# Products with w_ch2 by Strassen's algorithm inside each group of 288 tokens

## Chip, core and metric

The kernel runs on one core of a Trainium2 chip. The metric is the device time of one execution in microseconds (us). The kernel before takes 1440.85 us (median of 3 runs, 1440.07 to 1442.34). The core has five engines that work side by side: TensorE (PE, products into the PSUM banks), VectorE (DVE), ScalarE (ACT), GpSimd (POOL), and SyncE (SP), which here only issues DMA.

## What is computed

Attention with a threshold, over 8 batches, 8 heads, 576 tokens and 64 dimensions a head, and then a feed-forward block on the 512 features of each token:

```python
scores = (q @ k.T) / 8
scores = where(scores >= max(scores) - tau, scores, -1e9)
attn = exp(scores - max(scores)); attn /= sum(attn) + 1e-9
x = (attn @ v), heads side by side                        # (8, 576, 512)
xn = (x - mean(x)) / sqrt(var(x) + 1e-6) * g_ln
out = x + maximum(xn @ w_ch1, 0) @ w_ch2                  # 512 -> 2048 -> 512
```

Everything is float32. The change concerns the last product, with w_ch2, of 2048 hidden values by 512 features.

## The kernel before

The 4608 tokens are worked in 16 groups of 288 (TOK), two to a batch. The attention of a batch is cut into 9 slots (SLOTS). A slot takes the scores of a pair of heads for 256 rows of queries (one slot of the nine takes the rows left over), in two PSUM tiles sc0 and sc1. The feed-forward products of a finished group are spread over the slots that follow, as filler between the slot's own products, in four portions ("quarters") per slot. Constants: NK = 4 blocks of 128 features, ND = 16 blocks of 128 hidden values, B = 8, HP = 4.

A product of 128 x 128 weights is issued as two matmuls of 64 output columns each:

```python
    def product(out, lhsT, rhs, **flags):
        for h in range(2):
            r = slice(64 * h, 64 * h + 64)
            nc.tensor.matmul(out[r], lhsT=lhsT[:, r], rhs=rhs, **flags)
```

The attention of a slot: maxima (neg, on DVE), exponentials (ACT), threshold and sums (DVE), division (POOL), block transposes (DVE), and a way through memory that finishes the transposition (SP). From the second batch on all slots go this way.

```python
        # exponentials(): neg, thr, and es = att.tile(..., tag="e"), two buffers
            nc.vector.tensor_reduce(out=neg[:, i], in_=pairs[h], axis=AXL.X, op=ALU.max, negate=True)
            # ... thr on POOL ...
            nc.scalar.activation(es[:, i], blocks[i], func=AF.Exp, bias=neg[:, i : i + 1])
        # weights():
            nc.vector.scalar_tensor_tensor(out=es[:, i], in0=blocks[i], scalar=thr[:, i : i + 1],
                in1=es[:, i], op0=ALU.is_ge, op1=ALU.mult, accum_out=den[:, i : i + 1])
        nc.vector.reciprocal(den, den)
            nc.gpsimd.tensor_scalar(out=es[:, i], in0=es[:, i], scalar1=den[:, i : i + 1], ...)
        # turn_blocks(): two transposes per slot into et (one buffer), then to memory
                    nc.vector.transpose(et[...], es[:, 2 * h : 2 * h + 2]...)
            nc.sync.dma_start(out=scr[:, :, a]..., in_=et[32 * a : 32 * a + 32])   # 4 of them
        # fetch(), in the next slot:
        nc.sync.dma_start(out=em, in_=rows[: J * 128]...)
        nc.sync.dma_start(out=er[:64], in_=rows[J * 128 :])        # the tile "rest"
        # values_of(), in the next slot's last quarter: em and rest times v, into sc0's free columns
```

When a group's x is complete, its mean is taken by a product with a constant matrix, and DVE centres x:

```python
    def centre(g):
        xc = centred[g] = ffn.tile([128, NK, TOK], F32, tag="xc", bufs=1, name="xc")
        for c in range(NK):
            nc.vector.tensor_tensor(out=xc[:, c], in0=groups[g][:, c], in1=mean, op=ALU.subtract)
```

The feed-forward block of a group is a generator. ps_ff has two PSUM banks; p1, p2, mean, var and the segments of the change share them. Things for other engines that need not be issued at once are appended to the list aside, which the main loop empties four times per slot.

```python
    def ffn_steps(g):
        for d in range(ND):
            p1 = ps_ff.tile([128, TOK], F32, tag="ff", name="p1")
            for c in range(NK):
                product(p1, lhsT=w1_sb[c][:, d * 128 : (d + 1) * 128], rhs=xc[:, c], ...)
                # yield 1 after each: one step of the filler
            nc.scalar.activation(hidden[:, d], p1, func=AF.Relu)
            # d == 1: squares of xc into sq, summed on POOL; d >= 8: product var with avg_sb, and
            # root() by three steps on DVE: rb = 1 / sqrt(var + eps)
        for m in range(NK):
            p2 = ps_ff.tile([128, TOK], F32, tag="ff", name="p2")
            for d in range(ND):
                product(p2, lhsT=w2_sb[:, m, d], rhs=hidden[:, d], start=(d == 0), stop=(d == ND - 1))
            aside.append(lambda m=m, p2=p2: add_to_x(g, m, p2, rb))

    def add_to_x(g, m, p2, rb):
        o = ffn.tile([128, TOK], F32, tag="o", bufs=6, name="o")
        nc.vector.tensor_mul(o, p2, rb)
        nc.gpsimd.tensor_tensor(out=o, in0=o, in1=groups[g][:, m], op=ALU.add)
        aside.append(lambda: store(g, m, o))     # a DVE transpose into ot, then four DMA to out
```

The pace: ROOM gives the share of each quarter, and what is left of a group's steps is spread evenly until the next group is ready. Within a slot the order is: scores; neg; two exponentials; quarter 0; two exponentials; transposes of the next heads' q and k (kT, qT), if any; aside; quarter 1; weights(); aside; quarter 2; turn_blocks(); aside; quarter 3 with the values' product ahead of it; aside.

## Time and profile before

| engine | busy us | share of the span of 1438.0 us |
|---|---|---|
| PE | 1389.3 | 97% |
| DVE | 868.9 | 60% |
| POOL | 439.0 | 31% |
| ACT | 421.7 | 29% |

The page of the profile gives the busy time of each engine, the chain of work that ended last, and groups of instructions by line; the timeline lists instructions in order of time. A row of a group gives line, engine, operation, output and inputs, shape, count, busy time, the mean of one in ns, and the engine's idle time just before it with what ended it. In a timeline row the bracket at the end gives the idle time ahead of the instruction and what released it. The products with w_ch2 are named p<-hidden,w, those with w_ch1 p<-xc,w; the scores are sc<-kT,qT, the values sc<-em,v_in. In the last 20 us PE runs alone with the last group's products: 31.21 us for 256 records of p<-hidden,w, and the span ends some 6 us after them.

### The profile page before, as it was taken

What the parts mean: (1) busy time and instruction counts of PE and PEld (TensorE: products, weight loads), DVE (VectorE), ACT (ScalarE), POOL (GpSimd) and SP (SyncE); (2) the same over time, 40 slices, a digit from 0 to 9 for tenths busy, and PEclk for the clock granted to TensorE, in tenths of its full rate; (3) what the DMA queues carried; (4) which work ended last, traced back from release to release, by engine and by line L of the source; (5) the groups of instructions that cost most, each with busy time, mean ns of one, the idle gap of its engine ahead of it and who ended that gap; (6) DMA issues with size and microseconds to landing.
All of it is one profiled execution on the core that took longest, in us unless ns stands there. A gap on an engine that the chain in (4) does not pass through costs nothing.

```text
span 1438.0 us, 29661 instructions
## 1 busy us (share of the span) xinstructions
PE 1389.3 (97%) x12168; PEld 851.0 (59%) x12168; DVE 868.9 (60%) x1492; ACT 421.7 (29%) x818; POOL 439.0 (31%) x681
## 2 busy tenths in 40 slices
PE   4879999999999999999999999999999999999998
PEld 3655665655656555655556555565556555565664
DVE  5997957556665666566665565656665666655111
ACT  3886523132221313132221312213131222213020
POOL 2344432333323233232322333232332323222100
PEclk8999999999999999999999999999999999999999
DMA  9722456658755586557865577555875578455301
GB/s 223 176 69 83 90 137 157 168 136 168 178 145 145 144 185 166 142 134 168 184 156 145 146 160 168 144 145 144 175 179 146 130 168 185 135 145 137 79 6 17
DMA packets 466840, 205.12 MB, mean 143 GB/s; under 512 B 275024, under 2 KB 428368, under 8 KB 466704
## 3 DMA queue, kind: packets, MB, share of 16 engines
q1 hardware_dynamic: 461936, 202.64, 58.6%
q8 instruction: 95, 1.56, 0.5%
q10 hardware_dynamic: 4736, 0.59, 0.4%
q14 instruction: 41, 0.34, 0.1%
q0 software_dynamic: 32, 0.00, 0.0%
HBM read 119.41 MB, written 83.76 MB: 141 GB/s over the span
## 4 chain that ended last, share of the span: by engine, by line
PE 89%; DVE 5%; ACT 2%; DMA 2%; issue 1%; SPq 1%; POOL 0%; POOLq 0%; DVEq 0%; ACTq 0%
PE p L100 67%; PE sc L538 10%; PE sc L384 10%; DVE e L416 1%; PE tp L100 1%; DMA v_in<-in_v_dram 1%; DVE neg L398 1%; SPq L115 1%; ACT e L409 1%; PE mean L100 0%; DVE et L494 0%; DVE w L263 0%; PE var L100 0%; DMA qk_room<-in_q_dram 0%; ACT hidden L649 0%
## 5 line engine op out<-in xcount | busy, mean ns | idle before, releaser
L100 PE MATMUL p<-xc,w 128*64 128x288 f32 x4096 | 517.9, 408 | 6.6 <-ACT hidden L649 4.5
L100 PE MATMUL p<-hidden,w 128*64 128x288 f32 x4096 | 513.9, 407 | 0.0
L100 PEld LDWEIGHTS p<-xc,w 128*64 128x64 f32 x4096 | 292.6, 137 | 216.0 <-ACT hidden L649 14.5
L100 PEld LDWEIGHTS p<-hidden,w 128*64 128x64 f32 x4096 | 293.3, 137 | 200.6 <-issue 9.3
L398 DVE TENSOR_REDUCE neg<-sc 128x2 f32<-128x1152 f32 x144 | 188.8, 1353 | 252.1 <-PE sc L384 252.1
L409 ACT ACTIVATE e<-sc,neg 128x576 f32<-128x576 f32 x288 | 194.6, 742 | 261.3 <-DVE neg L398 255.9
L429 POOL TENSOR_SCALAR e<-e,den 128x576 f32<-128x576 f32 x252 | 188.3, 766 | 242.6 <-DVE den L420 242.6
L416 DVE SCALAR_TENSOR_TENSOR e<-sc,thr,e 128x576 f32<-128x576 f32 x288 | 219.1, 811 | 24.2 <-ACT e L409 24.2
L494 DVE STREAM_TRANSPOSE et<-e 128x1152 f32<-128x1152 f32 x112 | 153.6, 1375 | 78.2 <-POOL e L429 52.1
L649 ACT ACTIVATE hidden<-p 128x288 f32<-128x288 f32 x256 | 105.7, 414 | 284.7 <-PE p L100 282.9
L384 PE MATMUL sc<-kT,qT 64*128 64x384 f32 (+3 forms) x1024 | 150.0, 424 | 20.9 <-DVE e L416 10.8
L402 POOL TENSOR_SCALAR thr<-neg,low_sb 128x2 f32<-128x2 f32 x144 | 41.8, 291 | 352.9 <-DVE neg L398 344.0
L384 PEld LDWEIGHTS sc<-kT,qT 64*128 64x128 f32 x1024 | 94.1, 190 | 77.9 <-issue 26.8
L538 PE MATMUL sc<-em,v_in 128*64 128x256 f32 (+1 forms) x1408 | 131.1, 330 | 2.6 <-DVE sq L627 1.2
L555 ACT COPY x<-sc 128x256 f32<-128x256 f32 x60 | 22.3, 372 | 314.6 <-PE sc L538 289.6
L538 PEld LDWEIGHTS sc<-em,v_in 128*64 128x64 f32 x1408 | 86.2, 138 | 42.1 <-issue 1.7
L597 POOL TENSOR_TENSOR o<-o,x 128x288 f32<-128x288 f32 x64 | 51.6, 806 | 151.5 <-DVE o L596 151.5
L596 DVE TENSOR_TENSOR o<-p,rb 128x288 f32<-128x288 f32 x64 | 28.1, 439 | 103.1 <-PE p L100 102.5
L564 POOL TENSOR_TENSOR sum<-sum,x 128x256 f32<-128x256 f32 (+1 forms) x64 | 32.9, 514 | 76.8 <-ACT x L555 74.3
L655 POOL TENSOR_TENSOR sq<-sq 128x288 f32<-128x288 f32 x48 | 38.8, 807 | 42.1 <-ACT sq L653 39.6
L564 POOL TENSOR_TENSOR sum<-x 128x256 f32<-128x256 f32 (+1 forms) x32 | 16.2, 507 | 96.5 <-ACT x L555 55.1
L538 PE MATMUL sc<-rest,v_rest 128*64 128x256 f32 (+1 forms) x352 | 44.4, 329 | 0.0
(130 smaller groups left out, 713.9 us busy)
## 6 DMA issues: line engine op xcount, KB each, us to landing
scr<-et SPq DMA_DIRECT2D x252, 288.0 KB, 4.8
em<-scr SPq DMA_DIRECT2D x63, 1024.0 KB, 5.9
out_dram<-ot SPq DMA_DIRECT2D x256, 36.0 KB, 4.4
q_in<-in_q_dram SPq DMA_DIRECT2D x124, 72.0 KB, 3.3
k_in<-in_k_dram SPq DMA_DIRECT2D x120, 72.0 KB, 2.8
v_in<-in_v_dram SPq DMA_DIRECT2D x64, 128.0 KB, 4.4
rest<-scr SPq DMA_DIRECT2D x63, 128.0 KB, 5.9
w<-in_moe_w_ch_dram SPq DMA_DIRECT2D x10, 512.0 KB, 6.8
```

Source lines behind the costliest of these rows:

```text
L100: nc.tensor.matmul(out[r], lhsT=lhsT[:, r], rhs=rhs, **flags)
L384: nc.tensor.matmul(sc[h][64 * i : 64 * i + 64 if s == HP else 128, at : at + n], lhsT=ql[r] if s == HP else qT[r, half, j * 128 : (j + 1) ...
L398: nc.vector.tensor_reduce(out=neg[:, i], in_=pairs[h], axis=AXL.X, op=ALU.max, negate=True,)
L402: nc.gpsimd.tensor_scalar(out=thr[:, i], in0=neg[:, i], scalar1=-1.0, scalar2=low_sb, op0=ALU.mult, op1=ALU.add,)
L409: nc.scalar.activation(es[:, i], blocks[i], func=AF.Exp, bias=neg[:, i : i + 1])
L416: nc.vector.scalar_tensor_tensor(out=es[:, i], in0=blocks[i], scalar=thr[:, i : i + 1], in1=es[:, i], op0=ALU.is_ge, op1=ALU.mult, accum_o ...
L429: nc.gpsimd.tensor_scalar(out=es[:, i], in0=es[:, i], scalar1=den[:, i : i + 1], scalar2=1.0, op0=ALU.mult, op1=ALU.mult,)
L494: nc.vector.transpose(et[:, :, 64 * h : 64 * h + 64].rearrange("p n (j c) -> p j n c", j=2), es[:, 2 * h : 2 * h + 2].rearrange("p j (n c) ...
L538: nc.tensor.matmul(dst[64 * h : 64 * h + 64], lhsT=vt[:, c, h, :] if c < J else vr[:, h, :], rhs=pick(em[:, c] if c < J else er, hp, h), s ...
L564: nc.gpsimd.tensor_tensor(out=sums[g][:, cols], in0=x[:, 0, cols] if c == 1 else sums[g][:, cols], in1=x[:, c, cols], op=ALU.add,)
L597: nc.gpsimd.tensor_tensor(out=o, in0=o, in1=groups[g][:, m], op=ALU.add)
L649: nc.scalar.activation(hidden[:, d], p1, func=AF.Relu)
```

## The change

Strassen's algorithm (in Winograd's form) multiplies two matrices cut into 2 x 2 blocks by 7 block products in place of 8, at the price of sums and differences of blocks. Here w_ch2 is cut by halves of the output features and of the hidden values, and hidden by halves of the hidden values and of the tokens (early and late, 144 each). The first group (g = 0) stays as it was; from the second on (g >= 1) each group takes seven "segments" of 16 products with 144 moving columns. A segment accumulates two blocks of features in one PSUM bank, and ACT copies it out.

The sums of weights are made once, during the first products of group 1: s1 in place of a block of w_ch2, s2 and s3 in the staging tile of the weights' conversion, s4 in one of the two rooms for e (so the attention has a single room for e from then on). The differences of hidden (t1 to t4) are made per group, in place in hidden, by DVE (t1, t2) and POOL (t3, t4). POOL adds the seven results up (u2, u3, u4, 11, 12, 21, 22), DVE multiplies by rb, POOL adds x, and the result is transposed and stored as before. The steps' count and the places of the squares and of var within the first product are adapted. The aim is fewer products on the engine that is busiest.

```diff
@@ -88,6 +88,7 @@
     rests = [consts.tile([128, 4, 128], F32, name=f"rest{i}") for i in range(2)]
     v_rest = [consts.tile([128, 2, D], F32, name=f"v_rest{i}") for i in range(HP)]
     hidden = consts.tile([128, ND, TOK], F32, name="hidden")
+    e_room = [consts.tile([128, 4, S], F32, name=f"e{i}") for i in range(2)]
# ... the weights' staging tile is kept as self.stage ...
 
-    def exponentials():
+    def exponentials(n):
 
 
         neg = small.tile([128, 4], F32, tag="neg", name="neg")
         thr = small.tile([128, 4], F32, tag="thr", name="thr")
-        es = att.tile([128, 4, S], F32, tag="e", name="e")
+        es = e_room[(n + 1) % 2 if n < SLOTS else 0]
         for h in range(2):
             i = slice(2 * h, 2 * h + 2)
# ...
@@ -629,15 +630,47 @@
         if step < 2:
             aside.append(lambda: root(y, x, t, step + 1))
 
-    def ffn_steps(g):
-
+    HT, HD, HM = TOK // 2, ND // 2, NK // 2
+    early, late = slice(0, HT), slice(HT, TOK)
+    w2 = {
+        (i, j): w2_sb[:, HM * i : HM * i + HM, HD * j : HD * j + HD]
+        for i in range(2)
+        for j in range(2)
+    }
+    more = []
+
+    def differences():
+
+
+        flat = conversion.stage.rearrange("p a b -> p (a b)")
+        flat4 = e_room[1].rearrange("p a b -> p (a b)")
+        size = HM * HD * 128
+        for t in (flat[:, :size], flat[:, size : 2 * size], flat4[:, :size]):
+            more.append(t.rearrange("p (m d c) -> p m d c", m=HM, d=HD))
+        s2, s3, s4 = more
+        s1 = w2[1, 0]
+        for eng, out, a, b, op in (
+            (nc.gpsimd, s3, w2[0, 0], w2[1, 0], ALU.subtract),
+            (nc.vector, s1, w2[1, 0], w2[1, 1], ALU.add),
+            (nc.vector, s2, s1, w2[0, 0], ALU.subtract),
+            (nc.gpsimd, s4, w2[0, 1], s2, ALU.subtract),
+        ):
+            for m in range(HM):
+                for d in range(0, HD, 4):
+                    at = (slice(None), m, slice(d, d + 4))
+                    eng.tensor_tensor(out=out[at], in0=a[at], in1=b[at], op=op)
+                    yield
+
+    def first_part(g):
 
 
         xc = centred.pop(g)
-        rb = None
+        rb = sq = None
+        plain = g == 0
+        sums_of = differences() if g == 1 else iter(())
         for d in range(ND):
             while conversion.ended < 4 * (d // 4 + 1):
-                yield 0
+                yield 0, 0
             p1 = ps_ff.tile([128, TOK], F32, tag="ff", name="p1")
             for c in range(NK):
                 product(
@@ -645,35 +678,145 @@
                     start=(c == 0), stop=(c == NK - 1),
                 )
                 if c < NK - 1:
-                    yield 1
+                    yield 1, 1
             nc.scalar.activation(hidden[:, d], p1, func=AF.Relu)
-            yield 2
-            if d == 1:
+            next(sums_of, None)
+            yield 2, 1
+            if d == (1 if plain else 5):
                 sq = ffn.tile([128, NK, TOK], F32, tag="sq", bufs=1, name="sq")
                 nc.scalar.activation(sq, xc, func=AF.Square)
                 for c in range(1, NK):
                     nc.gpsimd.tensor_tensor(out=sq[:, 0], in0=sq[:, 0], in1=sq[:, c], op=ALU.add)
-            if d >= 8 and rb is None and (part or d == ND - 1):
+            if d >= (8 if plain else 11) and rb is None and (part or d == ND - 1):
 
                 var = ps_ff.tile([128, TOK], F32, tag="ff", name="var")
                 product(var, lhsT=avg_sb, rhs=sq[:, 0], start=True, stop=True)
                 rb = ffn.tile([128, TOK], F32, tag="rb", bufs=2, name="rb")
                 nc.scalar.activation(sq[:, 1], var, func=AF.Identity, bias=eps_sb)
                 aside.append(lambda: root(rb, sq[:, 1], sq[:, 2]))
-                yield 1
+                yield 1, 1
+        for _ in sums_of:
+            pass
+        return rb
+
+    def second_plain(g, rb):
         for m in range(NK):
             p2 = ps_ff.tile([128, TOK], F32, tag="ff", name="p2")
             for d in range(ND):
                 while conversion.ended <= conversion.n1 + 4 * m + d // 4:
-                    yield 0
+                    yield 0, 0
                 product(
                     p2, lhsT=w2_sb[:, m, d], rhs=hidden[:, d],
                     start=(d == 0), stop=(d == ND - 1),
                 )
                 if d < ND - 1:
-                    yield 2
+                    yield 2, 1
             aside.append(lambda m=m, p2=p2: add_to_x(g, m, p2, rb))
-            yield 2
+            yield 2, 1
+
+    def second_quarters(g, rb):
+
+
+
+
+        s2, s3, s4 = more
+        b11, b12 = hidden[:, :HD, early], hidden[:, :HD, late]
+        b21, b22 = hidden[:, HD:, early], hidden[:, HD:, late]
+        y = ffn.tile([128, NK, TOK], F32, tag="sq", bufs=1, name="y")
+        part_of = lambda t, i, j: t[:, HM * i : HM * i + HM, (early, late)[j]]
+        y11, y12, y21, y22 = (part_of(y, i, j) for i in range(2) for j in range(2))
+        done = set()
+
+        def later(*calls):
+            for what, fn, *args in calls:
+
+                def go(what=what, fn=fn, args=args):
+                    fn(*args)
+                    done.add(what)
+
+                aside.append(go)
+
+        def need(*what):
+            while not done.issuperset(what):
+                run_all(aside)
+
+        def by_fours(eng, out, in0, in1, op):
+            for d in range(0, HD, 4):
+                at = (slice(None), slice(d, d + 4))
+                eng.tensor_tensor(out=out[at], in0=in0[at], in1=in1[at], op=op)
+
+        def segment(weights, rhs, out=None):
+            bank = ps_ff.tile([128, HM, HT], F32, tag="ff", name="seg")
+            for d in range(HD):
+                for m in range(HM):
+                    at, end = (d, m), (HD - 1, HM - 1)
+                    product(
+                        bank[:, m], lhsT=weights[:, m, d], rhs=rhs[:, d],
+                        start=at == (0, 0), stop=at == end,
+                    )
+                    if at != end:
+                        yield 2, 0.5
+            if out is None:
+                out = ffn.tile([128, TOK], F32, tag="o", bufs=6, name="o")
+                out = out.rearrange("p (m t) -> p m t", m=HM)
+            nc.scalar.copy(out, bank)
+            return out
+
+        def add(out, a, b):
+            side.tensor_tensor(out=out, in0=a, in1=b, op=ALU.add)
+
+        def finish(i, j):
+
+            z = part_of(y, i, j)
+            r = rb[:, (early, late)[j]].unsqueeze(1).to_broadcast([128, HM, HT])
+            nc.vector.tensor_tensor(out=z, in0=z, in1=r, op=ALU.mult)
+            add(z, z, part_of(groups[g], i, j))
+
+        def give(i):
+            for m in range(HM * i, HM * i + HM):
+                store(g, m, y[:, m])
+
+        side = nc.gpsimd
+        later(("t3", by_fours, nc.gpsimd, b12, b22, b12, ALU.subtract))
+        yield from segment(w2[0, 0], b11, y11)
+        later(("t2", by_fours, nc.vector, b11, b11, b12, ALU.add))
+        yield 2, 0.5
+        p2 = yield from segment(w2[0, 1], b21)
+        later(("t4", by_fours, nc.gpsimd, b21, b21, b11, ALU.subtract))
+        yield 2, 0.5
+        need("t3")
+        p7 = yield from segment(s3, b12)
+        yield 2, 0.5
+        need("t2")
+        yield from segment(s2, b11, y21)
+        need("t4")
+        later(
+            ("t1", by_fours, nc.vector, b11, b22, b11, ALU.subtract),
+            ("u2", add, y21, y21, y11),
+            ("11", add, y11, y11, p2),
+        )
+        yield 2, 0.5
+        p4 = yield from segment(w2[1, 1], b21)
+        later(("done11", finish, 0, 0))
+        yield 2, 0.5
+        need("t1", "u2", "11")
+        p5 = yield from segment(w2[1, 0], b11)
+        later(
+            ("u4", add, y12, y21, p5), ("u3", add, y21, y21, p7), ("22", add, y22, y21, p5),
+            ("21", add, y21, y21, p4), ("done22", finish, 1, 1), ("done21", finish, 1, 0),
+            ("hi", aside.append, lambda: give(1)),
+        )
+        yield 2, 0.5
+        p3 = yield from segment(s4, b22)
+        later(
+            ("12", add, y12, y12, p3), ("done12", finish, 0, 1),
+            ("lo", aside.append, lambda: give(0)),
+        )
+        yield 2, 0.5
+
+    def ffn_steps(g):
+        rb = yield from first_part(g)
+        yield from (second_quarters if g else second_plain)(g, rb)
 
 
 
@@ -681,7 +824,8 @@
 
 
     ROOM = (0.6, 1.0, 1.25, 0.35)
-    STEPS = 1 + NK * ND * 2
+    STEPS = [1 + NK * ND * 2] + [1 + NK * ND * 2 - NK * ND // 8] * (NG - 1)
+    ends = [sum(STEPS[: i + 1]) for i in range(NG)]
     queue = []
     issued = part = 0
     owed = 0.0
@@ -708,14 +852,14 @@
         if not queue:
             return
         at = QUARTERS * n + i
-        g = issued // STEPS
+        g = sum(issued >= e for e in ends)
         left = sum(ROOM[t % QUARTERS] for t in range(at, ready(g + 1))) if g + 1 < NG else 0
-        owed += ((g + 1) * STEPS - issued) * ROOM[i] / left if left > 0 else 8
+        owed += (ends[g] - issued) * ROOM[i] / left if left > 0 else 8
 
 
         got = 1 if i in (0, QUARTERS - 1) else 2
         while queue and (owed >= 0.5 or got == 1 and i in (0, QUARTERS - 1)):
-            got = next(queue[0], None)
+            got, cost = next(queue[0], (None, 0))
             if got is None:
                 queue.pop(0)
                 got = 1
@@ -723,8 +867,8 @@
                 owed = 0.0
                 break
             else:
-                issued += 1
-                owed -= 1
+                issued += cost
+                owed -= cost
 
     def group_ready(g):
         first = divmod(ready(g), QUARTERS)
@@ -759,7 +903,7 @@
 
         scores(b, s)
         run(n, -1)
-        rest = exponentials()
+        rest = exponentials(n)
         es, thr = next(rest)
         run(n, 0)
         conversion.fetch(2)
```

More of the change, by code (lines that the diff above doesn't have):

```diff
@@ L201, in __init__ @@
             x_room = ffn.tile([128, NK, TOK], F32, tag="x", bufs=3, name="x_room")
-            stage = consts.tile([128, 8, WC], F32, name="stage")
+            stage = self.stage = consts.tile([128, 8, WC], F32, name="stage")
             et = att.tile([128, NB, 128], F32, tag="et", bufs=1, name="et0")
```

## Prediction

> **What bounds the kernel now.** I began with the page's share of each engine and its chain of work that ended last. TensorE (PE) is busy 97% of the span and is 89% of the chain; no other engine passes 60%.
>
> ```profile
> PE 1389.3 (97%) x12168; PEld 851.0 (59%) x12168; DVE 868.9 (60%) x1492; ACT 421.7 (29%) x818; POOL 439.0 (31%) x681
> PE p L100 67%; PE sc L538 10%; PE sc L384 10%; DVE e L416 1%; PE tp L100 1%; DMA v_in<-in_v_dram 1%; DVE neg L398 1%; SPq L115 1%; ACT e L409 1%; PE mean L100 0%; DVE et L494 0%; DVE w L263 0%; PE var L100 0%; DMA qk_room<-in_q_dram 0%; ACT hidden L649 0%
> L100 PE MATMUL p<-hidden,w 128*64 128x288 f32 x4096 | 513.9, 407 | 0.0
> ```
>
> The third line is the product the change replaces: 4096 records (each call of product issues two matmuls, each of which leaves two records), 256 per group of 288 tokens, never waiting. From 150 us on PE is busy in at least 97% of every stretch I asked for (199.3 of 200 us between 600 and 800). PE time saved there is saved in the whole, unless something makes PE wait.
>
> For the spacing of matmuls I used the chain in order of time and the timeline, because the mean of 407 ns is the latency of a pipelined instruction. Columns: start, length, what, count.
>
> ```profile
> 410.20 12.28 PE p L100 x100
> 440.99 2.33 PE sc L538 x80
> 26.55 3.77 PE L100 MATMUL tp<-diag,e 128*64 128x128 f32 x64
> ```
>
> With 288 moving columns a record takes 12.28/100 = 122.8 ns; with 64 columns 2.33/80 = 29.1 ns; with 128 columns (3.77 - 0.27 of the last one's own latency)/63 = 55.6 ns. All three load new weights for each record. So a record costs columns/2.4 GHz plus 2.3 to 2.8 ns, and weight loads stay hidden down to 64 columns.
>
> Then the slack of the attention work beside PE. One slot starts at 780.27 (scores); the next starts at 799.75, its values' product at 813.83:
>
> ```profile
> 780.27 2.21 PE L384 MATMUL sc<-kT,qT 64*128 64x384 f32 x16
> 785.59 1.55 DVE L579 TENSOR_TENSOR xc<-x,mean 128x288 f32<-128x288 f32 x4
> 790.41 2.92 POOL L429 TENSOR_SCALAR e<-e,den 128x576 f32<-128x576 f32 x4 [4.83 <-DVE den L420]
> 791.91 2.83 DVE L494 STREAM_TRANSPOSE et<-e 128x1152 f32<-128x1152 f32 x2 [1.26 <-POOL e L429]
> 794.76 3.80 SPq L500 DMA_DIRECT2D scr<-et  x4
> 802.07 2.62 DVE L398 TENSOR_REDUCE neg<-sc 128x2 f32<-128x1152 f32 x2 [6.97 <-PE sc L384]
> 802.55 0.38 SPq L509 DMA_DIRECT2D em<-scr  x1
> 804.78 0.41 ACT L649 ACTIVATE hidden<-p 128x288 f32<-128x288 f32 x1
> 813.83 1.90 PE L538 MATMUL sc<-em,v_in 128*64 128x256 f32 x16
> ```
>
> Two slacks are visible. VectorE (DVE) waits 6.97 us for the next scores after its transposes. And from the end of et (794.74) the way through memory takes 7.81 us to the issue of em, 5.9 us (median in the issue list) to its landing, and rest is issued 0.43 us later: about 14.1 us, to 808.9. The product that reads it comes at 813.83, 4.9 us later.
>
> **The Trainium skill.** "TensorE: Matmul & The Clock Gate", section "Wait — 56ns, not 53.3ns?", gives columns/2.4 GHz plus about 2.5 ns for warm matmuls in a row; the trace agrees (122.8, 55.6, 29.1 ns). The same page, "Back-to-back issue gap", says that pairs of weight load and matmul sustain only about 81 ns at 128 columns; the trace disagrees (55.6 ns), and I follow the trace. "SBUF — State Buffer", "Who interferes with whom", says that a DVE instruction with two SBUF inputs contends with a GpSimd (POOL) instruction that reads SBUF; the trace agrees: root's steps take 0.46 us alone and 0.88 to 0.92 us at 567 us, beside POOL's scaling of e. "PSUM — Partial Sum Buffer", "Engine vs sequencer instructions", says that the queues of ScalarE, VectorE and GpSimdE are strictly first in, first out; the trace agrees: a p1 begun at 801.90 is done after 16 records, near 804.1, but its Relu starts at 804.78, when the two exponentials ahead of it are through.
>
> **The change, part by part.**
>
> PE. Per group 4 x 16 products become 7 x 16 of half the columns: 256 records to 448, 288 columns to 144. At 144/2.4 + 2.4 = 62.4 ns that is 28.0 us in place of 256 x 122.8 = 31.4 us: 3.5 us less per group, 15 groups, **-52 us**. Seven eighths of the columns remain; the extra fixed 2.4 ns of 192 more records takes back 0.5 us of the ideal 3.9.
>
> Added elsewhere per group. ACT: 7 copies of a bank, 0.41 us each like hidden's row. POOL: 11 additions of 288 elements at 0.81 us (row L597) in place of 4, and 4 differences of 576 elements, 1.4 us each as an estimate from rows L564 and L597 (32 columns 0.28, 288 columns 0.81, so 2 ns a column): 11 us more. DVE: 4 differences of 576 (0.8 us like row L416) and 4 multiplications in place of 4: about 3.5 us more. Over 15 groups POOL goes to about 610 us, DVE to 920, ACT to 465. None can bound a span of 1400. What matters is where these stand in each engine's strict order, which I read from the built program.
>
> Slots in which an odd group ends (g = 3, 5, ... 13: six). DVE's order is now: maxima, xc, e, den, *three multiplications by rb*, et, four transposes; POOL's: four scalings of e, u4, u3, 22, 21, two additions of x, 12, one addition of x. The multiplications wait for POOL, so et waits behind them. From the slot's start, with the trace's times: den at 10.0, POOL's scalings to 13.1, then u4, u3, 22, 21 at 0.85 each (spacing of L655's chain) to 16.4, two additions of x to 18.1, 12 to 18.95; third multiplication to 19.5; et 19.5 to 22.3. Before, et ended at 14.5. It is 7.9 us late, against 4.9 us of slack through memory and 7 us before the next maxima (four transposes instead of one also sit there). Maxima start 2.4 us late; exponentials and then Relu follow in ACT's order, the first Relu 3.1 us after the maxima's start (804.78 - 802.07 gives 2.7, plus its 0.41), and with two PSUM banks the third p1 of the slot waits 1.9 us. The product with em then waits until 22.3 + 14.1 = 36.4, where PE without waits would be at 32.0. Total 4.5 us, 5 with contention: 6 x 5 = **+30 us**.
>
> Slots in which an even group ends (g = 2 to 12: six). Here xc stands behind the multiplications of 22 and 21, which wait for POOL's chain: DVE has xc at 21.05 where PE wants it at 20.6; the maxima come 1.65 us late, which costs the third p1 another 0.6; and t1, behind the transposes of kT and qT, is ready 0.2 us late for its segment. About 1.4 us: **+8 us**.
>
> End. After the last matmul before: multiplication, addition, transpose, four stores. After: copy, 12, multiplication, addition, two transposes, eight stores behind eight of the upper half, all in one queue at 0.45 us per issue (16 in the last 25 us, four of them in 1.82 us). About **+5 us**. Group 14's end outside attention (xc again behind POOL, 1.5), group 1's slot (2) and the weights' differences in group 1 (16 instructions beside PE, about 0.5): **+4 us**.
>
> The single room for e from slot 10 on costs nothing: in DVE's order both transposes of et already stand before the next maxima, on which the exponentials wait.
>
> Sum: 1440.85 - 52 + 30 + 8 + 5 + 4 = 1436. Each wait was counted in full at median landing times, so I lean a little lower: **1432 us**.
>
> **Rivals.**
> *All is hidden*: PE stays 99% busy, only the end costs: 1440.85 - 52 + 5 = 1394. For it: DVE's and POOL's idle time, and 7 us of slack in the slot shown. Against: POOL's eight additions in a row stand before et in the order.
> *Weight loads bind*: 7/4 as many loads, each used for half the columns. At 81 ns a record, 448 take 36.3 us, 4.9 more than before, +73 us: 1514. Against: 29.1 ns at 64 columns with a load each.
> *The late et is worse than counted*: contention lengthens POOL's chain by 2 to 3 us and DMA lands late: 12 x 2 us more, about 1460.
>
> **Range and chances.** The PE term is firm, within 4 us. The waits are a walk by hand through three queues, and could be half (1413) or half again (1455) of the 42 us. So 1410 to 1450. Faster by over 2% (below 1412) needs most waits to be absent: 0.15. Slower by over 2% needs the second or third rival in full: 0.05. Within 2%: 0.80.
>
> **What would show it.** Right: 448 seg records per group at 62 to 63 ns; PE's busy share falling from 97% to (1389 - 52)/1432, about 93%; waits of PE's p1 on Relu or xc, and of the values' product on em, after every odd group, about 5 us together; et in that slot ending near 22 us after its scores; DVE waiting for POOL at the multiplications. Wrong: a seg record at 65 ns or more, seg waiting for t1 to t4 by more than a microsecond, or no wait in those slots (then 1394).

## The result and the profile after

The changed kernel takes **1496.53 us** (median of 4 runs, 1493.05 to 1497.36) against 1440.46 us for the kernel before beside it (1436.34 to 1442.34). The ratio is 1.0389, 95% interval [1.0371, 1.0408]: 3.9% slower. 1432 us had been predicted, and 1410 to 1450 as the range.

The page of the changed kernel: the share of each engine, then the chain that ended last by engine and by line.

```profile
PE 1361.4 (91%) x15048; PEld 1008.2 (68%) x15048; DVE 934.4 (63%) x1560; ACT 459.4 (31%) x923; POOL 635.7 (43%) x854
PE 48%; DVE 18%; DMA 12%; POOL 9%; SPq 6%; issue 4%; ACT 2%; DVEq 0%; POOLq 0%; ACTq 0%
PE seg L101 17%; PE p L101 15%; PE sc L539 8%; PE sc L385 7%; DVE e L417 6%; DMA scr<-et 5%; DMA em<-scr 5%; POOL y L766 4%; POOL e L430 4%; DVE et L495 3%; SPq L501 2%; DVE neg L399 2%; SPq L116 2%; DVE xc L580 1%; PE tp L101 1%
```

PE does less (1389.3 to 1361.4 us), but its share falls from 97% to 91%. The chain by engine of the kernel before was

```profile
PE 89%; DVE 5%; ACT 2%; DMA 2%; issue 1%; SPq 1%; POOL 0%; POOLq 0%; DVEq 0%; ACTq 0%
```

Now PE has 48% of it. Of the rest, the lines shown give 27% to the path of the attention weights: maxima, thresholds and transposition (DVE neg, e, et), scaling (POOL e), the way through memory (scr, em), and the issue of scr in SyncE's queue (SPq, the queue of the DMA-issuing engine). POOL's sums of results (POOL y) have another 4%.

The chain in order of time has the new products in pure stretches (start, length, count):

```profile
1309.58 12.16 PE seg L101 x196
```

12.16/196 is 62.0 ns a record, where 62.4 was reckoned. So the products are as cheap as thought. The groups of PE by line show what they wait for; the column after the second bar is the idle time just ahead, with its releasers. The values' product in the kernel before, then after:

```profile
L538 PE MATMUL sc<-em,v_in 128*64 128x256 f32 (+1 forms) x1408 | 131.1, 330 | 2.6 <-DVE sq L627 1.2 <-DVE et L494 0.8 <-DVE sq L624 0.6
```

```profile
L539 PE MATMUL sc<-em,v_in 128*64 128x256 f32 (+1 forms) x1408 | 142.4, 348 | 53.2 <-DMA em<-scr 35.2 <-DVE rb L629 6.8 <-DVE et L495 5.9
```

The idle time ahead of this product grows from 2.6 to 53.2 us. (The releasers other than DMA are read with care. DVE's rb and sq have nothing to do with this product, and the waits put down to them fit em: the two that end at 587.58 and 685.26 end 5.8 and 6.3 us after em's issue, which takes 5.9 us to land, median of the page.) The list of waits of the changed kernel (who waited for whom, total us, times, longest) has the others:

```profile
PE p L101 <- DVE xc L580: 14.3, 8, 2.5
PE seg L101 <- ACT o L762: 7.2, 6, 1.2
PE seg L101 <- POOL hidden L746: 2.7, 1, 2.7
```

Why em is late shows in the timeline of the changed kernel, in a slot in which an odd group ends (it starts at 628.23 us) and in the one after it:

```profile
643.83 0.46 DVE L772 TENSOR_TENSOR y<-y,rb 128x288 f32<-128x288 f32 x1 [5.55 <-POOL y L766]
648.07 2.63 DVE L495 STREAM_TRANSPOSE et<-e 128x1152 f32<-128x1152 f32 x2
650.73 3.80 SPq L501 DMA_DIRECT2D scr<-et  x4
658.54 0.38 SPq L510 DMA_DIRECT2D em<-scr  x1
659.52 10.88 SPq L610 DMA_DIRECT2D out_dram<-ot  x16
661.88 2.82 DVE L495 STREAM_TRANSPOSE et<-e 128x1152 f32<-128x1152 f32 x2 [3.58 <-POOL e L430]
664.53 1.95 PE L539 MATMUL sc<-em,v_in 128*64 128x256 f32 x16 [2.81 <-DMA em<-scr]
670.51 3.89 SPq L501 DMA_DIRECT2D scr<-et  x4
678.97 0.45 SPq L510 DMA_DIRECT2D em<-scr  x1
685.26 1.95 PE L539 MATMUL sc<-em,v_in 128*64 128x256 f32 x16 [2.71 <-DVE rb L629]
```

Two different things stand here. First what was predicted: DVE's multiplication by rb waits 5.55 us for POOL, et behind it ends at 650.70, 22.5 us after the slot's start (22.3 predicted), and PE waits 2.81 us for em. Then what was not: in the next slot et is done at 664.70, 15.7 us after that slot's start (14.5 in the slot of the kernel before), but the write of scr is issued only at 670.51. SyncE's queue was busy until 670.40 with the group's 16 stores, 10.88 us of issuing. PE waits 2.71 us more, at 685.26, in a slot where VectorE was hardly late.

An even group's stores come as two rows of 8. The kernel before has such a row too, in the slot that the prediction shows, but early in it; it ends 5.9 us before et is done:

```profile
783.19 5.67 SPq L609 DMA_DIRECT2D out_dram<-ot  x8
```

In the changed kernel eight loads stand between the two rows (558.16 to 573.81 in all); et, done at 567.48, waits for its scr until 573.91, and PE waits 4.07 us at 587.58. Sorted by place, the 53.2 us are 19.1 in the six slots where an odd group ends, 12.6 in five slots behind a row of 16, 16.7 in five slots behind two rows of 8, and 4.8 elsewhere.

The difference of the two profiled spans, 1491.3 - 1438.0 = 53.3 us, can be put together from PE's side. The first line uses an experiment below in which the new products stand alone (PE busy 1339.3 us).

| part | us | from |
|---|---|---|
| fewer columns | -50.0 | PE busy 1389.3 to 1339.3 |
| the same 15048 records take longer | +22.1 | 1339.3 to 1361.4 |
| idle ahead of the values' product (em) | +50.6 | 2.6 to 53.2 |
| p1 waits for xc | +14.0 | 0.3 to 14.3 |
| segments wait for a bank's copy, for t3 | +9.9 | 7.2 + 2.7 |
| from the last matmul's end to the span's end | +6.8 | 6.27 to 13.05 |
| sum | +53.4 | |

### The profile page after: what moved, and what is told of

Its sections match the earlier page's. It is cut to its first block, busy times and chain, and to the rows that moved or that the text cites. A ratio compares the mean times of both kernels' runs of the same rounds, so it can differ in the third digit from the quotient of the medians.

```text
span 1491.3 us, 36015 instructions
## 1 busy us (share of the span) xinstructions
PE 1361.4 (91%) x15048; PEld 1008.2 (68%) x15048; DVE 934.4 (63%) x1560; ACT 459.4 (31%) x923; POOL 635.7 (43%) x854
## 4 chain that ended last, share of the span: by engine, by line
PE 48%; DVE 18%; DMA 12%; POOL 9%; SPq 6%; issue 4%; ACT 2%; DVEq 0%; POOLq 0%; ACTq 0%
PE seg L101 17%; PE p L101 15%; PE sc L539 8%; PE sc L385 7%; DVE e L417 6%; DMA scr<-et 5%; DMA em<-scr 5%; POOL y L766 4%; POOL e L430 4%; DVE et L495 3%; SPq L501 2%; DVE neg L399 2%; SPq L116 2%; DVE xc L580 1%; PE tp L101 1%
## 5 line engine op out<-in xcount | busy, mean ns | idle before, releaser
L101 PE MATMUL p<-xc,w 128*64 128x288 f32 x4096 | 524.3, 410 | 19.8 <-DVE xc L580 14.3
L101 PEld LDWEIGHTS p<-xc,w 128*64 128x64 f32 x4096 | 300.4, 138 | 226.8 <-issue 29.5
L430 POOL TENSOR_SCALAR e<-e,den 128x576 f32<-128x576 f32 x252 | 196.5, 796 | 213.4 <-DVE den L421 213.4
L101 PE MATMUL seg<-hidden,w 128*64 128x144 f32 x3840 | 249.2, 287 | 0.0
L101 PEld LDWEIGHTS seg<-hidden,w 128*64 128x64 f32 x3840 | 235.7, 137 | 12.4 <-issue 7.7
L539 PE MATMUL sc<-em,v_in 128*64 128x256 f32 (+1 forms) x1408 | 142.4, 348 | 53.2 <-DMA em<-scr 35.2
L385 PE MATMUL sc<-kT,qT 64*128 64x384 f32 (+3 forms) x1024 | 150.6, 425 | 20.1 <-DVE qT L345 10.1
L101 PE MATMUL seg<-hidden,stage 128*64 128x144 f32 x1920 | 123.4, 287 | 2.7 <-POOL hidden L746 2.7
L101 PEld LDWEIGHTS seg<-hidden,stage 128*64 128x64 f32 x1920 | 118.0, 137 | 6.5 <-POOL hidden L746 3.0
L556 ACT COPY x<-sc 128x256 f32<-128x256 f32 x60 | 22.3, 371 | 247.2 <-PE sc L539 241.1
L746 POOL TENSOR_TENSOR hidden<-hidden 128x576 f32<-128x576 f32 x60 | 85.1, 1437 | 23.0 <-ACT hidden L682 15.1
L772 DVE TENSOR_TENSOR y<-y,rb 128x288 f32<-128x288 f32 x60 | 35.5, 592 | 94.8 <-POOL y L766 94.8
L766 POOL TENSOR_TENSOR y<-y,o 128x288 f32<-128x288 f32 x90 | 79.3, 881 | 14.0 <-ACT o L762 9.3
```

The lines of the kernel that those rows point to most:

```text
L385: nc.tensor.matmul(sc[h][64 * i : 64 * i + 64 if s == HP else 128, at : at + n], lhsT=ql[r] if s == HP else qT[r, half, j * 128 : (j + 1) ...
L539: nc.tensor.matmul(dst[64 * h : 64 * h + 64], lhsT=vt[:, c, h, :] if c < J else vr[:, h, :], rhs=pick(em[:, c] if c < J else er, hp, h), s ...
L746: eng.tensor_tensor(out=out[at], in0=in0[at], in1=in1[at], op=op)
L766: side.tensor_tensor(out=out, in0=a, in1=b, op=ALU.add)
```

## The experiments

**Theory**: the product's saving is real; it is lost because the attention weights reach em too late, in two ways: the lateness of DVE, POOL and ACT that the prediction reckoned with, and a group's 16 stores, which now come together, in one row or in two of 8, and stand ahead of scr in SyncE's one queue. **Rivals**: PE itself is slower than its records tell; or the lateness of DVE and POOL is all of it, and merely dearer than reckoned.

In the recorded expectations, the mask is the attention weights on their way through et, scr and em. All times are medians; the ratio is that to the kernel before on the same chip, with its 95% interval.

| run | additions | stores | us | ratio |
|---|---|---|---|---|
| after | whole | together | 1496.5 | 1.0389 [1.0371, 1.0408] |
| k3_products_only | none | together | 1440.8 | 1.0010 [1.0002, 1.0018] |
| k5_products_spread | none | spread | 1429.8 | 0.9933 [0.9913, 0.9954] |
| k12_products_few_stores | none | 1 of 16 | 1396.4 | 0.9704 [0.9686, 0.9723] |
| k6_spread | whole | spread | 1457.9 | 1.0131 [1.0100, 1.0162] |
| k11_few_stores | whole | 1 of 16 | 1450.6 | 1.0071 [1.0047, 1.0096] |
| k18_tardy_few_stores | whole, reordered | 1 of 16 | 1417.9 | 0.9860 [0.9822, 0.9897] |
| k17_tardy | whole, reordered | spread | 1443.1 | 1.0029 [1.0017, 1.0040] |

### The products alone

*k3_products_only*: the seven segments run, but nothing around them; t1 to t4 and POOL's seven sums of results are left out, so the output isn't the product.

```diff
-        later(("t3", by_fours, nc.gpsimd, b12, b22, b12, ALU.subtract))
         yield from segment(w2[0, 0], b11, y11)
-        later(("t2", by_fours, nc.vector, b11, b11, b12, ALU.add))
-        p2 = yield from segment(w2[0, 1], b21)
+        yield from segment(w2[0, 1], b21)
# ... likewise t4, t1, u2, u3, u4, 11, 12, 21, 22; finish and give stay ...
```

> Seven segments per group as in the changed kernel, but without the differences of hidden (t1 to t4) and without the sums of results (u2, u3, u4, 11, 12, 21, 22): four multiplications by rb, four additions of x and the stores stay, so the output is not the product. Theory (the products do save 3.5 us per group, and waits ate it): 1390 to 1405 us. Rival (the segments are slower in themselves: weight loads, copies of banks on ACT, a lower clock): 1430 us or more.

Measured: 1440.8 us, inside the rival's range and 36 us above the theory's. The additions cost 56 us of the changed kernel's time, yet without any of them the kernel isn't faster than before. The idle ahead of the values' product is still 33.2 us here, and the timeline has the cause above: at 722.09 eight stores are issued in 3.93 us, scr, whose et was ready at 719.70, only at 726.12, and PE waits 4.25 us at 740.51. Whether the rival's reason, slow segments, has a part is settled by k12 below.

*k5_products_spread*: the same, and stores go out at most four at a time (one block of features), at the two places of a slot where all used to go.

```diff
+    def some_stores():
+        now = stores[:1]
+        del stores[:1]
+        for fn in now:
+            fn()
-        run_all(stores)
+        some_stores()
```

> The kernel with products only (no differences of hidden, no sums of results, so the output is not the product), its 16 stores of a group issued four at a time instead of 16 or 8 in a row. Theory C (SP's one queue: a group's results now end together, their stores stand in a row ahead of scr, and em comes late): the waits on em go, 1395 to 1410 us. Rival (the wait on em is memory traffic or DVE, not the queue): 1430 us or more.

Measured: 1429.8 us, 11 us less than k3 and practically at the rival's mark of 1430. Waits for em are still 21.4 us. Either spread stores still fill SyncE's queue or something else holds em.

*k12_products_few_stores*: k3's products, and of a group's 16 stores only the first is issued; 15 sixteenths of the output are not written.

```diff
-        for i in range(4):
+        for i in range(1 if m == 0 else 0):
```

> The seven products without the additions around them, and of a group's 16 stores only the first is issued (15 sixteenths of the output are not written). Queue theory: nothing stands before the mask's write but the loads, the waits for em fall under 8 us and the whole saving of the products shows: 1392-1408 us. Rival (PE's own records, the copies of the segments or the loads hold it): 1420 us or more.

Measured: 1396.4 us, inside the theory's range. Its page:

```profile
PE 1339.3 (96%) x15048; PEld 990.8 (71%) x15048; DVE 880.0 (63%) x1500; ACT 460.0 (33%) x923; POOL 458.7 (33%) x689
```

and the values' product among its groups:

```profile
L539 PE MATMUL sc<-em,v_in 128*64 128x256 f32 (+1 forms) x1408 | 132.2, 331 | 4.7 <-DVE et L495 2.8 <-DMA em<-scr 1.9
```

This is the 50 us of saving, shown: PE's records, their weight loads and the segments' copies cost what was reckoned. The rival that PE itself is slower falls. Between k12 and k3 nothing differs but 15 stores a group, and they cost 44 us. (The kernel before was not run with so few stores; its idle ahead of the values' product is 2.6 us with all of them.)

### The stores

*k2_stores_late*: after, with all waiting stores issued at one place behind the write of scr.

```diff
         conversion.fetch(2)
-        run_all(stores)
         second_part(n, 0)
# ...
+        run_all(stores)
         if s in (HP, 2 * HP):
             group_ready(2 * b + (s > HP))
```

> The changed kernel with the output stores issued once per slot, after the slot's stores to scr; the orders of DVE, POOL, ACT and PE stay. Theory B (stores of a whole group ahead of scr make em late in the following slots): about 7 us per pair of groups less, 1445 to 1460 us. Theory A alone: 1490 us or more.

Measured: 1539.0 us (1.0705 [1.0681, 1.0729]), 79 us above the theory's range and the opposite of what it was for. Nearly all stores now come in rows of 16 between scr and the read of em, which comes from the same queue: at 585.08 they take 10.06 us, em follows at 595.24, and PE waits 4.61 us at 601.84. Behind scr there is no room for ten us.

*k6_spread*: after, with k5's edit.

> The changed kernel with the stores four at a time, nothing else. Theory C as the larger part of the loss: 1445 to 1465 us. If the late et of the odd groups (DVE behind POOL's sums) is the larger part: 1480 us or more.

Measured: 1457.9 us, as the theory had it. Nothing but the grouping of the stores differs from after, and it is worth 39 us.

*b1_bunched*: the kernel before, with the stores of each group held until all four blocks are there; its computation is whole. (To hold them, ot gets four buffers of its own, and o has four in place of the six that both shared.)

```diff
+        ot = ffn.tile([128, TOK], F32, tag="ot", bufs=4, name="ot")
         nc.vector.transpose(ot, o)
-        stores.append(lambda: send(g, m, ot))
+        held.append(lambda: send(g, m, ot))
+        if len(held) == NK:
+            stores.extend(held)
+            held.clear()
```

> The kernel before (plain products), with the 16 stores of a group held back until its last block is transposed and then issued in a row, as Strassen's results make them come; the whole computation stays. Theory C: em comes late as in the changed kernel, 5 to 8 us per pair of groups, 1475 to 1495 us. Rival: within 5 us of 1440.

Measured: 1461.6 us (1.0157 [1.0133, 1.0181]). It lies between the two expectations: bunching alone does slow the old kernel, by 23 us, where 35 to 55 had been expected. The timeline of this kernel has the same order of events, without any Strassen:

```profile
389.28 2.82 DVE L494 STREAM_TRANSPOSE et<-e 128x1152 f32<-128x1152 f32 x2 [2.68 <-POOL e L429]
390.58 7.97 SPq L612 DMA_DIRECT2D out_dram<-ot  x16
398.65 3.89 SPq L500 DMA_DIRECT2D scr<-et  x4
412.83 1.95 PE L538 MATMUL sc<-em,v_in 128*64 128x256 f32 x16 [3.43 <-DMA em<-scr]
```

et is done at 392.10, scr goes out 6.55 us later, and PE waits for em. Only about every second row does this (six waits, 18.3 us). The row at 477.22 begins 9 us before its et is done, holds scr up by 0.7 us, and PE doesn't wait: what counts is where the row stands beside et.

*k9_products_act_queue*, *k8_act_queue*, *b2_act_queue*: if SyncE's queue is full, the stores can be issued from ScalarE's. In turn on k5, on k6 and on the kernel before:

```diff
-            nc.sync.dma_start(
+            nc.scalar.dma_start(
                 out=out[b, t * TOK : (t + 1) * TOK, f : f + 32].rearrange(
```

> The seven products without the additions, stores four at a time, and the stores issued from ScalarE's queue instead of SyncE's. Queue theory: the rest of the expected saving is missing because SyncE's one queue is full of issues in the slots where a group's results come, so the mask's write waits there; with the stores gone from it the waits for em fall from 21 us to under 6 us and the time falls from 1430 to 1400-1414 us. Rival (the loads alone fill the queue, or the issues cost ScalarE as much as they free): 1422 us or more.

> The changed kernel, whole, stores four at a time and from ScalarE's queue. Queue theory: the waits for em fall from 21 us to 8 us or less (VectorE's late et keeps some of them), and the time from 1458 to 1432-1446 us. Rival (the rest is VectorE's and GpSimd's own lateness, or ScalarE's issues now delay the copies of the segments): 1452 us or more.

> The kernel before with its stores issued from ScalarE's queue, nothing else moved. Queue theory: its mask has 4.9 us of slack and PE is never held by it, so the time stays within 5 us of 1440 us. Rival (SyncE's queue already costs the kernel before something): 8 us or more faster; a further one (issues on ScalarE delay the activations): 8 us or more slower.

Measured: 1497.9 (1.0418 [1.0385, 1.0452]), 1536.9 (1.0688 [1.0670, 1.0706]) and 1503.3 us (1.0450 [1.0433, 1.0467]). All three miss the theory and lie on the slow rivals' side, 65 to 79 us above k5, k6 and the kernel before. Of the kernel before with stores from ScalarE, the timeline (ACTq is ACT's issuing of DMAs), and from the list of waits what held SyncE's write of scr:

```profile
530.52 8.83 SPq L500 DMA_DIRECT2D scr<-et  x4
536.42 0.83 ACTq L609 DMA_DIRECT2D out_dram<-ot  x2
537.29 4.27 ACTq L609 DMA_DIRECT2D out_dram<-ot  x6
541.61 1.37 ACT L409 ACTIVATE e<-sc,neg 128x576 f32<-128x576 f32 x2 [3.87 <-DMA out_dram<-ot]
549.93 1.95 PE L538 MATMUL sc<-em,v_in 128*64 128x256 f32 x16 [1.87 <-DMA em<-scr]
SPq L500 <- DMA out_dram<-ot: 72.1, 18, 8.5
```

Eight issues stand between the second and the third exponential, which waits 3.87 us for them. So issuing a store takes its engine's time like an instruction does. But this is the smaller part: PE's waits for Relu rise only from 4.5 to 8.3 us, those for em to 37.5. The em awaited at 549.93 belongs to a scr begun at 530.52, before these issues. Its four writes took 8.83 us (3.80 at 794.76 in the kernel before), because SyncE stood still between them, by the profile for the stores' DMAs. In the four runs with stores from ScalarE, k10 below included, these waits are 72 to 137 us; in no other run are they over 0.6 us. Why scr, which shares no tile with the stores, waits for them is not shown. The Trainium skill's "Trainium Kernel Development and Optimization", "Key Constraints", says that issuing from several engines "only saves the sequencer's issue time" because the 16 DMA engines are the same; here even that saving did not show in the time. These runs thus don't tell whether SyncE's queue is the whole remainder; k12 does.

*k13_spread_behind*: k6, with one of the two places for four stores moved from ahead of scr to behind it.

```diff
         run_all(aside)
-        some_stores()
         tick(3)
# ...
             scr = turn_blocks(s, es)
+            some_stores()
             at_quarter(n + 1, 0, ...)
```

> All stores, at most four at a time, one place behind the mask's write instead of ahead of it, the other at the slot's start behind the read of the mask. If the place in the queue counts: 1442-1454 us, against 1458 with one of the two places ahead of the write. If the stores then only hold up the next read of the mask: within 4 us of 1458, or above it.

Measured: 1461.6 us (1.0155 [1.0129, 1.0182]): no gain. Moving this one place of four stores doesn't help; waits for em are 25.8 us against 21.0.

### The lateness of VectorE, GpSimd and ScalarE

*k11_few_stores*: after, whole but for the stores, of which only each group's first is issued (k12's edit).

> The changed kernel with its additions, only the first of a group's 16 stores issued. What is left of the loss is then the lateness of VectorE, GpSimd and ScalarE, which the prediction's sum put at 42 us on 1394 (1436, leaned to 1432). Theory (the sum was right but for SyncE's queue): 1418-1438 us, waits for em only in the slots after an odd group's end. Rival (their lateness is dearer than reckoned): 1448 us or more.

Measured: 1450.6 us, 13 us beyond the theory's 1438 and on the rival's side: the lateness is dearer than reckoned. It costs 54 us on k12 (57.2 between the two profiled spans), which are: idle ahead of the values' product 4.7 to 22.9 us, p1's waits for xc 0.3 to 13.7, a segment's wait for t3 2.7, the end 3.4, and 19.2 in which the same records take longer (1339.3 to 1358.5 us of PE busy). The segments' waits for ACT, 7.2 us, are the same in k12. As for places, the theory was right: 19.1 us of the waits for em stand in the six slots where an odd group ends, as much as in the changed kernel, and the 29 us in the slots behind the rows of stores are gone.

The longer records come in good part from the clock. Stretches of this kernel's timeline show it (start and end, length, PE busy, granted clock, DMA share, GB/s), around one wait of 3.82 us that ends at 823.02:

```profile
815.00:819.00 4.00, 4.00 (x36) 1.00 0.54 109
819.00:823.00 4.00, 0.20 (x2) 0.78 0.68 215
823.00:827.00 4.00, 3.98 (x20) 0.50 0.80 182
827.00:831.00 4.00, 4.00 (x30) 0.87 0.75 179
```

After the wait PE has half its clock for some four microseconds, and the product takes 3.68 us instead of 1.90. Summed over stretches of one us, as an estimate, PE busy times the missing share of the clock is 16.9 us in this kernel and 3.4 in k12, mostly 1.7 us a fall; so the clock is some 13 of the 19 us, and the rest is not accounted for. The Trainium skill's "TensorE: Matmul & The Clock Gate", "HAM oscillation — how this bites in real kernels", gives this as the price of idle gaps over about 3.4 us. The traces agree in kind but not on the mark: the clock falls to 0.57 after a wait of 2.24 us in the changed kernel and after 1.98 us in b1, and stays at 1.00 after 3.59 us in the changed kernel.

*k1_turn_first*: after, with the turning of the mask (et, scr) straight behind den, ahead of all other work of DVE in the slot.

```diff
         diags = weights(es, thr, blocks_go)
+        if blocks_go:
+            scr = turn_blocks(s, es)
         run_all(aside)
```

> The changed kernel with the transposes of et (and the stores to scr) issued straight after den, ahead of the waiting sums, multiplications and output transposes. Theory A (et stands behind POOL's sums in DVE's order): the wait of the values' product on em after each odd group (3 us) and part of what follows it goes, 1465 to 1480 us. Theory B (the output stores ahead of scr in the one DMA queue are the larger part): no more than 6 x 3 us, 1478 us or above.

Measured: 1486.6 us (1.0331 [1.0308, 1.0354]): 10 us, the rival's side. But the waits moved. Two groups of PE in this kernel:

```profile
L539 PE MATMUL sc<-em,v_in 128*64 128x256 f32 (+1 forms) x1408 | 139.1, 342 | 3.5 <-DVE et L495 2.1 <-DMA out_dram<-ot 0.8 <-DMA em<-scr 0.7
L101 PE MATMUL seg<-hidden,stage 128*64 128x144 f32 x1920 | 129.7, 294 | 24.8 <-DVE hidden L746 22.1 <-POOL hidden L746 2.7
```

The idle ahead of the values' product is gone (53.2 to 3.5 us). In its place segments wait 22.1 us for t2 (hidden), now behind et in DVE's order, and p1 24.8 us for xc. It put everything behind et, also what PE needs soon. The edit moves scr ahead of the stores as well, so the run doesn't tell theory A from theory B. It does show that the queue has places for all stores: rows of 16 still stand in it, now behind em and ahead of the next scr (at 658.93, 9.26 us, scr at 670.98), and rows of 8 between scr and em (at 582.81, 5.98 us, em at 588.88), and PE hardly waits for em.

*k4_reordered* and *k7_reordered_spread*: k1's edit and xc ahead of the multiplications, the first with k2's stores, the second with k6's.

```diff
-        run_all(aside)
         conversion.fetch(2)
         tick(5)
         run(n, 3)
+        run_all(aside)
```

> Both of the former, and xc of the next group issued ahead of the waiting multiplications where it comes in the last quarter. If orders of issue are the whole of the loss, most of 13 us per pair of groups goes: 1405 to 1425 us, below the kernel before. If something else holds (contention of DVE and POOL, the clock), 1440 us or more.

> The changed kernel with the stores four at a time, et (and its stores to scr) straight after den, and xc ahead of the waiting multiplications. If queue and orders of issue are all of it: 1405 to 1425 us. If something further holds (contention, clock, the copies of banks): 1440 us or more.

Measured: 1570.8 (1.0918 [1.0894, 1.0941]) and 1485.9 us (1.0328 [1.0282, 1.0374]): two misses. k4 carries k2's fault: 59.2 us of waits for em, up to 8.8 us long. In k7 waits for em fall to 10.3 us, but p1 waits 21.2 us for Relu, the segments 14.4 us for t2 and 10.1 us for their bank's copy. *k10_act_queue_xc_first* and *k14_spread_behind_xc_first* make only the move of xc, on k8 and on k13:

> As the run before it, and the centred tokens xc are computed ahead of the group's multiplications with rb, not behind them. If the 13 us of waits for xc are on the path: 8 to 15 us less than without the move, 1420-1436 us. If the multiplications put back cost as much by delaying et (multiplication, addition and transposition shifted later): within 4 us of it.

> The same with the centred tokens computed ahead of the multiplications with rb. The move took 5 us off with ScalarE's queue, where other waits covered it; here the 13 us of waits for xc should go: 5 to 12 us less than the run before it, 1434-1448 us. If the postponed multiplications delay the next mask as much: within 3 us of it.

Measured: 1531.7 (1.0651 [1.0635, 1.0667], 5 us less than k8) and 1465.5 us (1.0184 [1.0165, 1.0202], 4 us more than k13, whose single runs spread over 9 us). Waits for xc do fall (13.0 to 4.4 us in k14), but em rises from 25.8 to 31.8 us, Relu from 3.7 to 10.1. What is put off comes to lie before the next thing on the path.

*k18_tardy_few_stores* and *k17_tardy* sort the work by what PE needs: the differences t1 to t4 stay ahead of et; the multiplications by rb, the additions of x and the transposes of results come behind et and behind xc. k18 is this on k11, k17 on k6 with all stores.

```diff
-                aside.append(go)
+                (tardy if what[:4] in ("done", "hi", "lo") else aside).append(go)
# ...
         run_all(aside)
         conversion.fetch(2)
         tick(5)
         run(n, 3)
+        run_all(tardy)
```

> Only the first of a group's 16 stores issued; the multiplications with rb, the additions of x after them and the transpositions of results come behind the slot's turning of the mask and behind xc, the differences of activations stay ahead of it. Theory (these two waits are the lateness): waits for em fall from 20 us to under 8, those for xc from 14 to under 6, and the time from 1451 to 1400-1424 us. Rival (VectorE's and GpSimd's work is merely moved on, to the next maxima or the next differences): within 8 us of 1451.

> The same order with all stores, four at a time at two places of a slot. Theory: 1420-1440 us against 1458 without the new order. Rival: the em wait stays because SyncE's queue holds it anyway, 1448 us or more.

Measured: k18 1417.9 us, 33 us less than k11, as the theory had it; k17 1443.1 us, 15 us less than k6 and just outside what the theory expected. In k18 the group reads

```profile
L539 PE MATMUL sc<-em,v_in 128*64 128x256 f32 (+1 forms) x1408 | 133.9, 334 | 5.7 <-DVE rb L621 2.8 <-DMA em<-scr 2.6 <-DVE et L495 0.2
```

5.7 us in place of 22.9, with xc at 4.2 in place of 13.7: the two orders were three fifths of the lateness (33 of 54 us). With all stores the same group has

```profile
L539 PE MATMUL sc<-em,v_in 128*64 128x256 f32 (+1 forms) x1408 | 139.3, 343 | 18.3 <-DMA em<-scr 16.0 <-DVE rb L635 1.6 <-DVE sq L631 0.5
```

so the stores, spread as they are, still cost 25 us (1418 to 1443). k17 is the best whole version found: it beats after by 53 us and does not beat the kernel before (1.0029).

**What stays open.** The cost of spread stores depends on the rest: spread stores cost 33 us on the products alone (k12 to k5), 7 us on the changed kernel (k11 to k6) and 25 us on the sorted one. That a late et and a late queue hide each other in the same slot would explain it; no run separates this from a changed fall of the clock. Nor does a run separate what a store costs as an issue in the queue from what it costs as traffic beside scr and em on the DMA engines; only the share that comes from standing together (39 us, after to k6) is shown to be one of order. k1 bears on it: with all the stores' traffic but scr ahead of them PE waits 3.5 us for em, which speaks for the order, though its slots are longer. One issue for a block's four stores was not tried.

## Why the prediction was wrong

Step by step, as it put them:

- **PE, -52 us: right.** 62.0 ns a record, 50.0 us less PE busy, 1396 us where little else holds it. The rival *weight loads bind* is out.
- **Slots in which an odd group ends, +30: mechanism right.** et ended 22.5 us after the slot's start (22.3 predicted), DVE waited for POOL at the multiplications, PE for em. These six waits for em are 19.1 us with and without the stores, 3.2 each; the wait of the third p1 for Relu did not appear (3.8 us in all, 4.5 before).
- **Slots in which an even group ends, +8: mechanism right, too small.** xc cost 14.0 us, 1.8 for each of eight waits, where 0.45 was reckoned for xc itself. No wait for t1 appeared.
- **End, +5:** 6.8. Near the reckoning.
- **Not in the sum, of two kinds.** Segments wait 7.2 us for ACT's copy of a bank, six times 1.2, in k12's 1396 too. And the clock: a wait for em can be followed by some four us at half clock, so that its price is the wait and mostly 1.7 us more, some 13 us in k11. With the clock the lateness is 54 us on k12, where the sum had 47 and the lean left 43. (Half again of the 42 us of waits, on the sum's own 1394, is 1457 and not 1455; either lies outside the range that was given.)
- **The step that failed** is "What matters is where these stand in each engine's strict order". It was carried out for DVE, POOL, ACT and PE, and not for SyncE, whose order decides when scr and em are issued. The 7.81 us from et to the issue of em was taken over from a slot of the kernel before whose queue was free when et was done. The prediction knew the price of an issue (0.45 us, for the end) and that a group's results now come together, and used both for the end alone. In the changed kernel a row of 16 stores takes 9.6 to 11.5 us in the queue, twice the slack of 4.9 us that it had measured, and the waits for em behind the rows are 29 us; a group's stores but the first cost 44 us on the products alone (k12 to k3) and 46 us on the changed kernel (k11 to 1496.5).

So 1432 stood against 1451 for what the prediction looked at, and the 46 us on top are what it didn't. The chances followed the same blindness: "slower by over 2%" got 0.05 because it was thought to need the second or third rival *in full*. The third, a late et that is dearer than counted, has its part; the queue was no rival at all.

## What to carry to other kernels

A reordering that makes results come together makes their stores come together: lay out the DMA-issuing queue slot by slot, like any engine, with each issue as an instruction of its measured length, and look for what a critical transfer finds ahead of it. Moving the stores to a compute engine's queue was no way out here: it spent that engine's time, and the critical transfer waited all the same. Where PE is the bound, sort the other engines' work by when PE needs it, and count a wait of two to four us at some 1.7 us more than its length where the clock falls behind it.

## What was not expected of the hardware

- A DMA issue kept its queue busy for some 0.4 to 1 us: 16 stores of 36 KB 9.56 to 11.54 us on SyncE in the changed kernel, scr's four 3.80 us, em's one 0.38 us, six stores on ScalarE 4.27 us, during which the next exponential waited 3.87 us.
- With the stores on ScalarE's queue, SyncE's writes of scr waited for them, 72.1 us in all in the kernel before so changed; why stays open.
- The length of a wait doesn't tell whether the clock falls behind it. The same product takes 1.90 us after no wait; in the changed kernel

```profile
240.02 3.51 PE L539 MATMUL sc<-em,v_in 128*64 128x256 f32 x16 [2.24 <-DMA em<-scr]
839.22 1.95 PE L539 MATMUL sc<-em,v_in 128*64 128x256 f32 x16 [3.59 <-DMA em<-scr]
```

with a granted clock of 0.57 in the four us from 240 on and 1.00 in those from 839.2 on. What decides is not shown.
